# Threshold attention and a bilinear feed-forward layer on one core: transposes, normalisation and the read-back of turned weights put elsewhere in the slot

## The chip, the cores and the metric

The kernel runs on 1 core of one Trainium2 chip. The metric is the device time of one execution in microseconds (us), and the median of several executions is compared. Its engines are TensorE (PE in the profile; PEld is its weight load), VectorE (DVE), ScalarE (ACT), GpSimd (POOL) and SyncE (SP), which issues the DMA transfers. Each engine has its own list of instructions and works through it in order.

## What is computed

The first half is attention with a threshold: of each row of scores only those within tau of the row's maximum count. The second half is a feed-forward layer, the product of two linear maps, followed by a third.

```python
def _attn_ref(q, k, v, tau):            # (8, 8, 576, 64) each, tau = 0.02
    scale = 1.0 / np.sqrt(q.shape[-1])
    scores = scale * np.matmul(q, k.transpose(0, 1, 3, 2))
    thresh = np.max(scores, axis=-1, keepdims=True) - tau
    scores = np.where(scores >= thresh, scores, -1000000000.0)
    scores = scores - np.max(scores, axis=-1, keepdims=True)
    attn = np.exp(scores)
    attn = attn / (np.sum(attn, axis=-1, keepdims=True) + 1e-09)
    return np.matmul(attn, v).astype(np.float32)

def _moe_ref(x, w_a, w_b, w_out):       # x (4608, 512), d_ff 1536
    a = x @ w_a
    b = x @ w_b
    return (a * b @ w_out).astype(np.float32)
```

Between the two, the heads' outputs are put side by side: (8, 8, 576, 64) becomes (4608, 512).

## The kernel before

**Tiling.** Heads go in pairs, 32 of them (4 pairs for each of 8 batches). The 576 query rows of a pair are cut into five units, `u` = 0 to 3 with 128 rows of each of the two heads (two tiles `sc` of 128 x 576 scores) and `u` = 4 (`NT`) with the last 64 rows of both heads in one tile. That makes 160 units. Rows of `x` are gathered into blocks of 256, and each block is a piece of feed-forward work, a Python generator (`ffn`) that issues matmuls step by step.

**Slots.** The main loop (L877) has one slot `g` for each unit and three more. The Python order of a slot is the order on every engine: `keep_order` (L39) ties each instruction to the one before it on its engine. In slot `g`, for `g` > 8 (`BY_PE`), come one after the other:

- `scores` (L335): the matmuls of unit `g` into `sc`, then on VectorE the maxima `mx` (L354) and the thresholds `thr` (L355);
- `turn_blocks` (L436) for unit `g` - 1: VectorE transposes the normalised weights `tw` in place in blocks of 32 x 32 (L441), and SP writes them in four transfers to `swap`, a scratch tensor in DRAM (L452);
- `advance(PORTIONS[0] * pace)`: 30% of the slot's feed-forward matmuls;
- `weigh` (L365): ScalarE makes the exponentials out of `sc` (L374, L375), VectorE masks and sums them (L378), which frees the PSUM buffers of `sc`;
- transposes of coming q and k (`prep`), then `advance(PORTIONS[1] * pace)`: another 35%;
- in every second or third slot the product with v: `make_room`, then `weighted` (L528), whose matmuls (L478) read the turned weights `wT` of unit `g` - 3 and of the one before it; `settle` (L482) copies the result out, first ScalarE (L485), then VectorE (L487);
- `turn_back` (L455) for unit `g` - 2: SP reads the whole of `swap` into `wT` (L461). `wT` has two buffers, so it waits until the product before has read its own;
- `convert_first` (L227), while weights are still being converted (until about 155 us of the span): two operations of ScalarE for each piece of a weight matrix;
- `reciprocal` (L383, VectorE, L389 and L391; while weights are converted ScalarE adds the small constant, L387) and `normalise` (L394, ScalarE, L397);
- loads of coming q, k and v, stores, and the other 35% of the feed-forward matmuls.

**Joins.** Each feed-forward tile in PSUM is copied out by ScalarE or combined by VectorE (L629 to L645, L689, L691, L467, L468), in the order in which its matmuls were issued.

**Buffers.** All tiles in PSUM, scores, feed-forward and products, share four buffers of two banks (`banks`, L126). `tw` has three buffers, `swap` three, `wT` two.

The first eight units go another way (`turn_pe`: TensorE transposes, and the normalisation is part of it); the change doesn't touch them.

Of the kernel before, what the change touches and what calls it, by code (L numbers as in the profile page):

```python
# [23 lines left out]
BY_PE = 8  # L24
# [28 lines left out]
def kernel(  # L53
# [278 lines left out]
    def prep_copy(mT, tp):  # L332
        nc.vector.tensor_copy(mT.rearrange("p (c k) -> p c k", c=2), tp)

    def scores(i, u):  # L335
        qT, kT = prepared[i]["q" if i < HP else "q1" if u > 1 else "q0"], prepared[i]["k"]
        base = HALF if i >= HP and u > 1 else 0
        n = 2 if u < NT else 1
        sc = [banks(SH, "sc") for _ in range(n)]
        each = [(c, t, j) for c in range(2) for t in range(n) for j in range(2)]  # L340
        if units.index((i, u)) < BY_HEAD:
            each.sort(key=lambda x: x[2])
        for c, t, j in each:
            r = slice(j * D, (j + 1) * D)
            o = t if u < NT else 1 - j
            q0, to = (u * P + t * D if u < NT else MAIN) - base, slice(o * D, (o + 1) * D)
            nc.tensor.matmul(sc[j if u < NT else 0][to, c], qT[r, q0:q0 + D],  # L347
                             kT[r, c * SH:(c + 1) * SH], start=True, stop=True)
        mx = small.tile([P, 2], FP32, tag="mx", name="mx")
        thr = small.tile([P, 2], FP32, tag="thr", name="thr")  # L350
        bias = small.tile([P, 2], FP32, tag="bias", name="bias")
        for j in range(n):
            c = slice(j, j + 1)
            nc.vector.tensor_reduce(mx[:, c], sc[j], axis=AX.XY, op=ALU.max)  # L354
        nc.vector.tensor_scalar(thr[:, 0:n], mx[:, 0:n], cut, None, op0=ALU.subtract)  # L355
        scored[i, u] = (sc, thr, bias, mx)
# [37 lines left out]
    def normalise(i, u):  # L394
        ws, rcp = weights[i, u]
        for j, w in enumerate(ws):
            nc.scalar.activation(w, w, AF.Copy, scale=rcp[:, j:j + 1])  # L397
# [38 lines left out]
    def turn_blocks(i, u):  # L436

        ws, _ = weights.pop((i, u))
        t = whole.pop((i, u))
        for w in ws:  # L440
            nc.vector.transpose(w, w)  # L441
        if u < NT:
            swap = scratch.tile([G, P, NSLOT * Q], FP32, tag="swap", name="swap")
        else:
            swap = scratch.tile([2, P, NSLOT * Q], FP32, tag="swapt", name="swap")
        swaps[i, u] = swap
        for g in range(G):
            if u < NT:
                to, n = swap[g], G
            else:  # L450
                to, n = swap[g % 2, (1 - g // 2) * D:(2 - g // 2) * D], 2
            nc.sync.dma_start(to.rearrange("(r p) e -> p r e", p=Q),  # L452
                              t[g * Q:(g + 1) * Q, 0:n * NSLOT].rearrange("p (r s) e -> p r (s e)", r=n))

    def turn_back(i, u):  # L455

        swap = swaps.pop((i, u)).rearrange("g p e -> p g e")
        if u < NT or i < HP:
            turned[i, u] = turned_tile()
            n = G if u < NT else 2  # L460
            nc.sync.dma_start(turned[i, u][:, 0:n].rearrange("p g s e -> p g (s e)"), swap)  # L461
        else:
            for y in range(2):
                nc.sync.dma_start(turned[i, 2 + y][:, G].rearrange("p s e -> p (s e)"), swap[:, y])
# [343 lines left out]
    def advance(cols):  # L808
        running["owed"] += cols
        while running["owed"] > 0:  # L810
            if running["ffn"] is None:
                exchange_blocks()
                if not blocks:
                    running["owed"] = 0.0
                    return
                if len(blocks[0][0]) == 4 and state["first"] == 3:
                    first_sums(3)
                running["ffn"] = ffn(*blocks.pop(0))
                running["left"] = cost()
            step, rest, whole = next(running["ffn"], (None, 0, 0))  # L820
            if step == 0:
                running["owed"] = 0.0
                return
            if step is None:
                running["ffn"] = None
                state["through"] += 1
            else:
                running["owed"] -= step
                running["left"] -= step
                running["done"] = running["done"] + step if rest else 0  # L830
                running["rest"] = rest
                running["room"] = min(ROOM, whole // 2)
# [44 lines left out]
    for g in range(len(units) + PV_LAG):  # L877
        written = len(pending)
        state["converted"] = state["added"]
        here = g < len(units)  # L880
        converting = bool(early.get(g)) or bool(early.get(g - 1))
        if here:
            i, u = units[g]
            scores(i, u)
        exchange_blocks()
        pace = (PACE if g > BY_PE else PACE_EARLY) * BLOCK_COLS
        if g > BY_PE:
            pace = min(pace, backlog() / (min([a for a in arrivals if a > g] + [len(units) + PV_LAG + 1]) - g))
        pace += NSLOT * S / 2 / (NT + 1) + CATCH_UP * max(backlog() - BLOCK_COLS, 0)
        if 2 <= g < BY_PE + 2:  # L890
            weighted_unit(*units[g - 2])
            running["owed"] -= NSLOT * P // 2
        if g < 3:
            prep_copy(*prep_pe(g + 1, "q"))
        convert_rest(g, 0)
        if g == 3:
            for c in range(0, NSUM - 2 * CW + 1, 2 * CW):
                extra.append(sums_u32[:, c:c + 2 * CW].rearrange("p (f w) -> p f w", w=2))
        load_weights(RAWS)
        if g > BY_PE and g <= len(units):  # L900
            turn_blocks(*units[g - 1])
        if g > BY_PE:
            advance(PORTIONS[0] * pace)
        if here:
            weigh(i, u)
        if here and g < BY_PE:
            reciprocal(i, u, nc.vector)
        if 0 < g <= BY_PE:
            turn_pe(*units[g - 1])
        if g < 3:  # L910
            prep_copy(*prep_pe(g + 1, "k"))
        for p in range(HP, NPR):
            for name, d in (("q0", 2), ("k", 1), ("q1", 1)):
                if g == (second if name == "q1" else first)[p] - d:
                    prep(p, name)
        if g > BY_PE:
            advance(PORTIONS[1] * pace)
            n = g - PV_LAG
            if BY_PE <= n < len(units) and part(*units[n]):
                make_room()  # L920
                weighted(*part(*units[n]))
                running["owed"] -= NSLOT * width(*part(*units[n])) // 2
            if BY_PE + 1 < g <= len(units) + 1:
                turn_back(*units[g - 2])
        for n in early.get(g, [])[:1]:
            convert_first(n)
            convert_clamp(n)
        if here and g < BY_PE:
            diagonals(i, u)
        elif here:  # L930
            reciprocal(i, u, nc.scalar if converting else nc.vector)
            normalise(i, u)
        convert_rest(g, 1)
        if g <= BY_PE:
            advance(pace)
        convert_rest(g, 2)
        for n in early.get(g, [])[1:]:
            convert_first(n)
            convert_clamp(n)
        load_weights(RAWS)  # L940
        for p in range(HP, NPR):
            for name, d in (("q0", 4), ("k", 3), ("q1", 3)):
                if g == (second if name == "q1" else first)[p] - d:
                    load(p, name)
        for p in range(1, NPR):
            if g == first[p] - 1:
                load_v(p)
        if BY_PE <= g < BY_PE + HP:
            load_v(g - BY_PE, again=True)
        store(written)  # L950
        if g > BY_PE:
            advance(PORTIONS[2] * pace)
            advance(PORTIONS[3] * pace)

        if not converting and not state["sums"]:
            state["slots"] = state.get("slots", 0) + 1
            for n in {1: (0,), 2: (1,), 3: (2,)}.get(state["slots"], ()):
                for z in range(2):
                    weight_sums(n, z)
            if state["slots"] >= 3 and state["through"]:  # L960
                for z in range(2):
                    weight_sums(3, z)
                state["sums"] = True
        if g > first[HP] + 1 and not converting and state["first"] < 3:
            first_sums(state["first"])
# [37 lines left out]
```

## Time and profile before

| | |
|---|---|
| runs | 1473.37, 1474.51, 1476.1 us, median 1474.51 |
| profiled execution | 1469.17 us, span 1467.4 us |
| mean granted clock of TensorE | 0.996 |
| bytes read and written in HBM | 128.58 MB, 89.65 MB |
| chain that ended last | PE 81%, DVE 9%, DMA 4%, issue 2%, ACT 2% |

The groups of instructions that the change touches (name of what is written and read, number, busy us and mean ns of one; then the idle time of the engine ahead of them and what ended most of it):

| line, engine | what | number | busy, one | idle before |
|---|---|---|---|---|
| L354 DVE | mx<-sc | 288 | 205.2, 749 | 106.2, PE sc L347 |
| L441 DVE | tw<-tw | 272 | 196.0, 754 | 0.8, ACT tw L397 |
| L378 DVE | tw<-sc,thr,tw | 288 | 224.2, 800 | 14.1, ACT tw L375 |
| L397 ACT | tw<-tw,rcp | 272 | 197.8, 769 | 221.9, DVE rcp L391 |
| L375 ACT | tw<-sc,bias,scalars | 288 | 239.7, 832 | 9.9, ACT bias L374 |

And the transfers (number, KB each, median us from issue to landing): swap<-tw 480 of 144 KB, 2.6 and 128 of 72 KB, 1.8; wT<-swap 120 of 576 KB, 4.5, 56 of 144 KB, 2.6, and 4 of 288 KB, 3.3. SP waited 330.0 us for L441 before writes of swap and 102.5 us for products before reads of it.

A table of groups is read so: busy time is what an engine spends; idle time ahead of a group costs something only where another engine waits for that group in turn.

### The profile page before, as it was taken

What the parts mean: (1) busy time and instruction counts of PE and PEld (TensorE: products, weight loads), DVE (VectorE), ACT (ScalarE), POOL (GpSimd) and SP (SyncE); (2) the same over time, 40 slices, a digit from 0 to 9 for tenths busy, and PEclk for the clock granted to TensorE, in tenths of its full rate; (3) what the DMA queues carried; (4) which work ended last, traced back from release to release, by engine and by line L of the source; (5) the groups of instructions that cost most, each with busy time, mean ns of one, the idle gap of its engine ahead of it and who ended that gap; (6) DMA issues with size and microseconds to landing.
All of it is one profiled execution on the core that took longest, in us unless ns stands there. A gap on an engine that the chain in (4) does not pass through costs nothing.

```text
span 1467.4 us, 70219 instructions
## 1 busy us (share of the span) xinstructions
PE 1404.0 (96%) x31136; PEld 1224.5 (83%) x31136; DVE 1020.5 (70%) x2295; ACT 678.8 (46%) x1259; POOL 490.4 (33%) x678
## 2 busy tenths in 40 slices
PE   5779999999999999999999999999999999999998
PEld 4667687788978788899889978789898879989998
DVE  6888687778776877776757777677767786644314
ACT  5877455445544554544444545344544454331011
POOL 2764703333161606042425233241516060605000
PEclk9999999999999999999999999999999999999999
DMA  9977677678656775767545866377746776450000
GB/s 206 217 198 209 159 178 193 170 165 205 176 142 160 183 199 139 178 158 174 138 129 126 193 166 162 101 165 187 184 126 153 173 180 169 120 138 17 3 17 17
DMA packets 325056, 222.82 MB, mean 152 GB/s; under 512 B 169616, under 2 KB 308880, under 8 KB 324752
## 3 DMA queue, kind: packets, MB, share of 16 engines
q1 hardware_dynamic: 322384, 217.73, 60.1%
q8 instruction: 245, 4.01, 1.2%
q10 hardware_dynamic: 2368, 0.59, 0.2%
q14 instruction: 59, 0.48, 0.1%
HBM read 128.58 MB, written 89.65 MB: 149 GB/s over the span
## 4 chain that ended last, share of the span: by engine, by line
PE 81%; DVE 9%; DMA 4%; issue 2%; ACT 2%; SPq 1%; POOL 1%; DVEq 0%; ACTq 0%
PE pab L683 33%; PE po L728 18%; PE pab L622 11%; PE pv L478 9%; PE sc L347 9%; DVE mx L354 2%; DMA wT<-swap 2%; DVE tw L441 1%; DVE tw L378 1%; SPq L452 1%; PE po L774 1%; DVE low L255 1%; DVE xT L487 0%; POOL h L697 0%; POOL xU L502 0%
## 5 line engine op out<-in xcount | busy, mean ns | idle before, releaser
L397 ACT ACTIVATE tw<-tw,rcp 128x576 f32<-128x576 f32 x272 | 197.8, 769 | 221.9 <-DVE rcp L391 221.9
L354 DVE TENSOR_REDUCE mx<-sc 128x1 f32<-128x576 f32 x288 | 205.2, 749 | 106.2 <-PE sc L347 104.5
L375 ACT ACTIVATE tw<-sc,bias,scalars 128x576 f32<-128x576 f32 x288 | 239.7, 832 | 9.9 <-ACT bias L374 0.2
L378 DVE SCALAR_TENSOR_TENSOR tw<-sc,thr,tw 128x576 f32<-128x576 f32 x288 | 224.2, 800 | 14.1 <-ACT tw L375 13.0
L728 PE MATMUL po<-wo_sb,h 64*64 64x256 f32 x3264 | 217.0, 377 | 5.3 <-DVE t L640 5.2
L588 POOL TENSOR_TENSOR t<-u,t 128x512 f32<-128x512 f32 x14 | 17.8, 1275 | 542.1 <-ACT t L629 502.0
L441 DVE STREAM_TRANSPOSE tw<-tw 128x576 f32<-128x576 f32 x272 | 196.0, 754 | 0.8 <-ACT tw L397 0.8
L347 PE MATMUL sc<-kT,qT 64*64 64x288 f32 x2016 | 188.1, 404 | 2.4 <-DVE tw L378 1.5
L478 PE MATMUL pv<-wT,vm 64*64 64x160 f32 (+3 forms) x5184 | 183.6, 273 | 6.4 <-DMA wT<-swap 3.5
L728 PEld LDWEIGHTS po<-wo_sb,h 64*64 64x64 f32 x3264 | 159.1, 133 | 34.8 <-DVE t L640 6.4
L683 PE MATMUL pab<-xS,wa_sb 64*64 64x256 f32 (+1 forms) x2560 | 177.3, 366 | 1.8 <-issue 1.8
L478 PEld LDWEIGHTS pv<-wT,vm 64*64 64x64 f32 x5184 | 164.7, 134 | 17.0 <-issue 7.3
L683 PE MATMUL pab<-xS,wb_sb 64*64 64x256 f32 (+1 forms) x2560 | 176.2, 366 | 0.9 <-issue 0.9
L697 POOL TENSOR_TENSOR h<-h 128x256 f32<-128x256 f32 x168 | 117.7, 736 | 165.7 <-PE po L728 162.2
L683 PE MATMUL pab<-xT,wa_sb 64*64 64x256 f32 (+1 forms) x2304 | 156.1, 366 | 6.1 <-ACT wo_sb L242 1.8
L728 PE MATMUL po<-sums_u,h 64*64 64x256 f32 x2448 | 158.5, 376 | 0.6 <-DVE h L645 0.6
L683 PE MATMUL pab<-xT,wb_sb 64*64 64x256 f32 (+1 forms) x2304 | 156.9, 365 | 1.6 <-DVE h L691 1.0
L683 PEld LDWEIGHTS pab<-xS,wa_sb 64*64 64x64 f32 x2560 | 130.5, 133 | 18.9 <-issue 2.2
L683 PEld LDWEIGHTS pab<-xS,wb_sb 64*64 64x64 f32 x2560 | 131.1, 133 | 16.5 <-issue 1.6
L728 PEld LDWEIGHTS po<-sums_u,h 64*64 64x64 f32 x2448 | 118.2, 133 | 22.8 <-DVE h L645 1.0
L347 PEld LDWEIGHTS sc<-kT,qT 64*64 64x64 f32 x2016 | 111.2, 133 | 28.7 <-issue 6.3
L683 PEld LDWEIGHTS pab<-xT,wa_sb 64*64 64x64 f32 x2304 | 114.8, 134 | 22.1 <-ACT wo_sb L242 2.0
(119 smaller groups left out, 2003.8 us busy)
## 6 DMA issues: line engine op xcount, KB each, us to landing
swap<-tw SPq DMA_DIRECT2D x480, 144.0 KB, 2.6
wT<-swap SPq DMA_DIRECT2D x120, 576.0 KB, 4.5
vm<-in_v_dram SPq DMA_DIRECT2D x128, 72.0 KB, 3.1
swap<-tw SPq DMA_DIRECT2D x128, 72.0 KB, 1.8
kT<-in_k_dram SPq DMA_DIRECT2D x112, 72.0 KB, 4.3
wT<-swap SPq DMA_DIRECT2D x56, 144.0 KB, 2.6
out_dram<-kept SPq DMA_DIRECT2D x30, 256.0 KB, 4.0
raw<-in_moe_w_a_dram SPq DMA_DIRECT2D x18, 256.0 KB, 6.6
```

Of the source, the lines that this page charges most:

```text
L347: nc.tensor.matmul(sc[j if u < NT else 0][to, c], qT[r, q0:q0 + D], kT[r, c * SH:(c + 1) * SH], start=True, stop=True)
L354: nc.vector.tensor_reduce(mx[:, c], sc[j], axis=AX.XY, op=ALU.max)
L375: nc.scalar.activation(wb[j], sb[j], AF.Exp, bias=bias[:, j:j + 1], scale=e_scale)
L378: nc.vector.scalar_tensor_tensor(out=wv, in0=sb[j], scalar=thr[:, j:j + 1], in1=wv, op0=ALU.is_ge, op1=ALU.mult, accum_out=sums[:, j:j + 1])
L397: nc.scalar.activation(w, w, AF.Copy, scale=rcp[:, j:j + 1])
L441: nc.vector.transpose(w, w)
L478: nc.tensor.matmul(pv[c * D:(c + 1) * D, y], vm[rows, s], wT[y](rows, s), start=(s == 0), stop=(s == NSLOT - 1))
L588: (nc.vector if state["over"] else nc.gpsimd).tensor_tensor(*a, **kw)
L622: nc.tensor.matmul(pab[c * D:(c + 1) * D, r, y * P:(y + 1) * P], w[k][rows, w0:w0 + D], moving[k][rows], start=(k == 0), stop=(k == HP - 1))
L683: nc.tensor.matmul(pab[c * D:(c + 1) * D, r], w[rows, f // n, k, fs + c * D:fs + (c + 1) * D], moving, start=(k == 0), stop=(k == H - 1))
L697: (nc.vector if state["over"] else nc.gpsimd).tensor_tensor(*a, **kw)
L728: nc.tensor.matmul(po[c * D:(c + 1) * D, r, y], ht[rows, t0:t0 + D], other[rows, f], start=(f == 0), stop=(f == NF // 2 - 1))
```

## The change

Four edits belong together. The transposes of the unit before (`turn_blocks`, with its four writes of `swap`) are issued inside `scores`, after the matmuls and ahead of the maxima. They leave their place after `load_weights`, so their writes are now issued ahead of the loads of weights in the slot. The reciprocal and the normalisation of a unit are issued ahead of the product with v, `turn_back` and `convert_first` in slots after 8, instead of after them; slot 8 keeps the old place. And `turn_back` reads `swap` in `n` transfers, one for each group of 32 rows (four, or two for the units of 64 rows of the first four pairs), instead of one. The matmuls and GpSimd's operations keep their order.

```diff
-    def scores(i, u):
+    def scores(i, u, meanwhile):
...
             nc.tensor.matmul(sc[j if u < NT else 0][to, c], qT[r, q0:q0 + D],
                              kT[r, c * SH:(c + 1) * SH], start=True, stop=True)
+        meanwhile()
         mx = small.tile([P, 2], FP32, tag="mx", name="mx")
...
             n = G if u < NT else 2
-            nc.sync.dma_start(turned[i, u][:, 0:n].rearrange("p g s e -> p g (s e)"), swap)
+            for y in range(n):
+                nc.sync.dma_start(turned[i, u][:, y].rearrange("p s e -> p (s e)"), swap[:, y])
...
+        def turn():
+            if g > BY_PE and g <= len(units):
+                turn_blocks(*units[g - 1])
+
         if here:
             i, u = units[g]
-            scores(i, u)
+            scores(i, u, turn)
+        else:
+            turn()
         exchange_blocks()
...
         load_weights(RAWS)
-        if g > BY_PE and g <= len(units):
-            turn_blocks(*units[g - 1])
         if g > BY_PE:
             advance(PORTIONS[0] * pace)
...
         if g > BY_PE:
             advance(PORTIONS[1] * pace)
+            if here:
+                reciprocal(i, u, nc.scalar if converting else nc.vector)
+                normalise(i, u)
             n = g - PV_LAG
...
-        elif here:
+        elif here and g == BY_PE:
             reciprocal(i, u, nc.scalar if converting else nc.vector)
             normalise(i, u)
```

## The prediction

> **What bounds the kernel now.** I read the busy times first, then the table by stretches of time, then the waits of TensorE, then the order of time around two slots.
>
> ```profile
> PE 1404.0 (96%) x31136; PEld 1224.5 (83%) x31136; DVE 1020.5 (70%) x2295; ACT 678.8 (46%) x1259; POOL 490.4 (33%) x678
> ```
>
> PE is busy in 1404.0 of 1467.4 us: at most 63.4 us can be had from waits. The change leaves PE's own list as it is, so nothing else can move. The next table (stretch, length, then busy us of PE, PEld, DVE, ACT, POOL, clock, DMA) says where the 63.4 us lie.
>
> ```profile
> 0.00:62.00 62.00, 41.00 (x796) 34.13 (x796) 43.76 (x105) 39.71 (x82) 26.84 (x39) 0.94 1.08 214
> 62.00:125.00 63.00, 49.50 (x1458) 43.62 (x1459) 55.63 (x119) 46.97 (x94) 39.59 (x43) 1.00 0.84 219
> 125.00:400.00 275.00, 264.58 (x5536) 221.26 (x5537) 214.50 (x488) 147.05 (x270) 91.49 (x109) 1.00 0.71 177
> 400.00:800.00 400.00, 395.66 (x8819) 345.71 (x8819) 288.08 (x652) 188.06 (x344) 138.45 (x202) 1.00 0.63 157
> 800.00:1270.00 470.00, 461.81 (x10270) 402.39 (x10266) 338.72 (x769) 223.85 (x410) 156.75 (x230) 1.00 0.65 161
> ```
>
> 34.5 us of idle lie before 125 us, 10.4 + 4.3 + 8.2 = 22.9 us from there to 1270, the rest in the tail, which has no attention work. The change acts from slot 9 on, whose scores start at 86.5 us in the order of time. So about 23 us, and part of the 13.5 us of the second row, are in reach. The waits of PE from 125 us on (what waits, for whom: us, times, longest):
>
> ```profile
> PE po L728 <- DVE t L640: 5.2, 5, 1.7
> PE pv L478 <- DMA wT<-swap: 3.5, 3, 2.2
> PE pab L622 <- DVE h L691: 2.7, 3, 1.2
> PE sc L347 <- DVE tw L378: 2.3, 2, 1.5
> ...
> PE pab L622 <- DVE u L631: 1.8, 2, 1.1
> ```
>
> The reader is to see that the two large sorts are a join on VectorE that comes late and turned weights that come late. The order of time shows why a join can be late (start, duration; L354 maxima, L441 transposes, L378 masked sums, L389/L391 reciprocal, L487 settle):
>
> ```profile
> 531.10 0.59 DVE L487 COPY xT<-pv 64x128 f32<-64x128 f32 x2 [2.41 <-ACT xT L485]
> 531.72 0.17 DVE L389 TENSOR_SCALAR sums<-sums 128x2 f32<-128x2 f32 x1
> 531.93 0.17 DVE L391 RECIPROCAL rcp<-sums 128x2 f32<-128x2 f32 x1
> 532.01 1.40 DVE L354 TENSOR_REDUCE mx<-sc 128x1 f32<-128x576 f32 x2
> ...
> 539.18 1.42 DVE L354 TENSOR_REDUCE mx<-sc 128x1 f32<-128x576 f32 x2 [1.38 <-PE sc L347]
> 540.64 0.23 DVE L355 TENSOR_SCALAR thr<-mx,scalars 128x2 f32<-128x2 f32 x1
> 540.77 1.43 DVE L441 STREAM_TRANSPOSE tw<-tw 128x576 f32<-128x576 f32 x2
> 542.13 0.78 DVE L378 SCALAR_TENSOR_TENSOR tw<-sc,thr,tw 128x576 f32<-128x576 f32 x1
> ```
>
> There are two sorts of slot. After a slot without product VectorE sits idle for the scores (1.38 us here). After a slot with a product it comes from the settle and the reciprocal and is late itself, with no idle time.
>
> **What the Trainium skill says.** "PSUM — Partial Sum Buffer", section Engine vs sequencer instructions: the queues of ScalarE and VectorE are strict FIFO. The trace agrees: the reciprocal at 531.93 stands behind a settle that waited 2.41 us. "DMA: Bandwidth & Descriptors", section Issuing engines are not separate DMA queues: all transfers share the 16 DMA engines, so cutting one in four adds no bandwidth; its section Rules for kernel authors puts mostly overhead below 64 KB. The quarters are of 144 KB, and such ones land in 2.6 us here, the 576 KB one in 4.5.
>
> **Part 1, transposes to the front.** The same 272 x 754 ns of VectorE. In 72 waits VectorE idles 104.5 us before the maxima (L354 waits for L347), 1.45 us each: one pair of transposes (1.43 us). There they cost nothing, and what stood behind them, the joins of the first portion, comes 1.43 us earlier. The masked sums gain less, since they need the exponentials: from the maxima's start 0.79 to the first bias, then to the end of the second exponential 2.99 us (523.62 to 526.61), so the second masked sum starts at 3.0 instead of 1.42 + 0.23 + 1.43 + 0.75 = 3.8. In the other half of the slots, where VectorE is late, maxima start about 1.43 - 0.4 = 1.0 us later (0.4 is the reciprocal that left, part 2), joins 0.4 us earlier, the second masked sum 0.3 us later. Behind the transposes SP issues four writes of swap (1.76 us for four); they start 0.4 to 1.9 us earlier.
>
> The change adds a wait: the transposes now need the normalisation of the slot before, and behind them stand maxima, exponentials, and the release of the score banks. Before it is covered (L441 waited 0.8 us in all). The new round from maxima to maxima: 3.0 to the second masked sum, 1.26 from there to the normalisation (249.66 to 250.92), 0.75 for its first half, then both transposes 1.5: 6.5 us. Slots last 6 to 10.5 us; of the 142 after slot 16, 60 are under 7.8.
>
> **Part 2, reciprocal and normalisation ahead of the product.** On VectorE two small operations (0.35 to 0.4 us) leave the stretch between settle and maxima; on ScalarE 1.44 us of normalisation go ahead of the settle copy (0.27). Cover: PE's product, about 2 us. If masked sums are late the cover is gone and settle, then transposes, wait: 3.0 + 1.26 + 1.44 + 0.3 + 0.6 + 1.45 = 8.05 us for that round. With 0.6 us for one join between masked sum and reciprocal in each of the two slots, a pair then takes 6.5 + 8.05 + 1.2 = 15.75 against 15.0 for two slots of 7.5. The four PSUM buffers absorb about 1 us (an estimate: a second masked sum ends at 536.5, the next scores start at 537.8). In slots 9 to 16 ScalarE also converts weights (two to three pieces, 1.2 us each); the first piece, which filled its wait for the masked sum, now stands behind the normalisation: up to 1.2 us later per slot. Against it, the reciprocal no longer stands behind that piece (VectorE waited 1.61 us at 94.7). I take 0 for these slots; ends -2 and +6.
>
> **Part 3, four transfers.** 120 transfers become 480 (four others become eight): 364 more issues at 0.44 us = 160 us of SP's queue, 1.3 us a slot. Behind them stand loads and the writes of swap; SP issues in 64% of the densest stretch and still waits 330 us for transposes, so I cost this at nothing; without that cover a slot's writes start up to 1.3 us late, once in two slots. The last quarter is issued 1.3 us after the first and lands 2.6 later: 3.9 against 4.5. With part 1, weights are there 1 to 2.5 us earlier. PE waits on more semaphores before a product: the trace has no case; between nothing and 0.1 us for 60 products, I take 1 us, ends 0 and 5.
>
> **Sum.** Gains: of 5.2 for joins L640, the wait at 941 us lies in a slot with 1.79 us of idle (1.4), the other four give 0.35 each (1.4): 2.8. Of L691/L631 (4.5), the wait at 386 us goes whole (1.2), others 0.4: 2.4. Late weights 3.5 of 3.5. Score banks 0.5 of 2.3. Together 9.2. Losses: new round in tight slots 3 (ends 0 and 14), semaphores 1, conversion 0. Net -5.2: the profiled execution of 1469.2 us (span 1467.4) goes to about 1464. The median shown is 1474.5, 5.3 above it, and I take the same difference there: 1469.5.
>
> **Rivals.**
> 1. Stalls only move: a join that comes early lets PE run to the next bank that is not free. For it: 81% of the chain is PE, and few waits are over 1.5 us. Against it: the waits are single, with long quiet stretches between. Gain 9.2 less 3 and less half of the rest: about 1472.5 to 1475, no change.
> 2. The round decides (slower). Transposes wait at the front for ScalarE, which waits for VectorE. Price: 0.75 us for each pair of tight slots; 60 such slots are 30 pairs, 22 us, less a third that the buffers absorb: +15. Conversion adds +4, and of the gains only late weights (3.5) remain. 1474.5 + 15.5 = 1490 at full price, half of it 1482. It decides where a round with its join exceeds the slot, that is under about 7.8 us. For it: the normalisation ends up to 1.9 us after the scores in slots behind a product. Against it: that was behind the settle, and moves with part 2.
> 3. Nearly all waits in reach go (18 of 23): 1457. Against it: half the slots gain only 0.35 us.
> 4. The quarters don't start sooner than the whole, since both wait for the same release by the product (102.5 us of SP's waiting). Then 2 of the 3.5 us stay: 1471.5. It is inside the forecast.
>
> **Chances.** Forecast with rival 4: 0.42, rival 3: 0.06, rival 1: 0.20, rival 2: 0.32. What this measurement can tell from no change is 0.2%, 2.9 us. Part of the forecast lies within it, so faster is 0.44, same 0.23, slower 0.33. The range leaves out rival 3 and the dear half of rival 2: 1461 to 1486. The forecast's own range is 1464 to 1473.
>
> **What would show it.** Right: idle before L354 falls from 106 to under 50 us, and L441 waits for ScalarE or SP's wait for L441 shrinks; PE's waits for L640 fall to about 2.5 and for wT to under 1; 364 more reads of swap, landing in about 2.6 us. The forecast is wrong if L441 shows tens of us of waiting for L397, if PE waits for L378 before scores or products grow beyond 5 us, or if PE's busy time itself changes, which nothing here predicts.

## The result, and the profile after

The changed kernel takes 1501.76 us (1499.83 to 1502.21, four runs) against 1474.9 us (1473.37 to 1476.1): a ratio of 1.018, 95% interval 1.0163 to 1.0198. It is 27 us slower, where 5 us faster was forecast. The profiled execution took 1501.73 us, its span is 1499.9 us, 32.5 more than before: the profiled execution of the kernel before, at 1469.17 us, was faster than the median, so the two traces differ by some 5 us more than the medians do.

From the page of the changed kernel: the busy times, the chain that ended last, and the groups that the change touches. The functions stand one to two lines further down in this kernel: L355 are the maxima, L379 the masked sums, L442 the transposes, L398 the normalisation.

```profile
PE 1420.4 (95%) x31136; PEld 1229.5 (82%) x31136; DVE 1035.2 (69%) x2295; ACT 682.5 (46%) x1259; POOL 491.4 (33%) x678
...
PE 65%; DVE 14%; ACT 6%; DMA 6%; SPq 5%; issue 4%; POOL 0%; DVEq 0%; ACTq 0%; POOLq 0%
...
L398 ACT ACTIVATE tw<-tw,rcp 128x576 f32<-128x576 f32 x272 | 198.2, 771 | 246.6 <-DVE rcp L392 246.3
L379 DVE SCALAR_TENSOR_TENSOR tw<-sc,thr,tw 128x576 f32<-128x576 f32 x288 | 232.2, 816 | 70.8 <-ACT tw L376 53.2
...
L442 DVE STREAM_TRANSPOSE tw<-tw 128x576 f32<-128x576 f32 x272 | 197.8, 761 | 40.3 <-ACT tw L398 38.4
...
L355 DVE TENSOR_REDUCE mx<-sc 128x1 f32<-128x576 f32 x288 | 201.5, 734 | 20.3 <-PE sc L347 20.1
...
wT<-swap SPq DMA_DIRECT2D x544, 144.0 KB, 2.9
```

The chain is where to look first. PE's share of it fell from 81% to 65%; VectorE, ScalarE, transfers and SP's queue took over. The idle time ahead of the maxima fell from 106.2 to 20.3 us, as forecast. But VectorE now waits elsewhere: 70.8 us ahead of the masked sums (14.1 before) and 40.3 us ahead of the transposes (0.8 before).

The waits of TensorE after (what waits, for whom: us, times, longest), and those of SP's queue:

```profile
PE pv L480 <- DMA wT<-swap: 8.2, 7, 2.1
PE sc L347 <- issue: 7.4, 7, 2.5
...
PE sc L347 <- DVE tw L379: 5.1, 9, 1.4
PE po L730 <- DVE kept L470: 4.5, 3, 1.9
...
PE po L730 <- DVE t L642: 2.2, 3, 0.9
```

```profile
SPq L463 <- PE pv L480: 142.1, 44, 7.8
SPq L453 <- DVE tw L442: 126.5, 57, 8.0
```

The reader is to see which forecasts held and which did not: the wait for the join L640 (now L642) fell from 5.2 to 2.2 us, but the wait for turned weights rose from 3.5 to 8.2, and a new one for the join of `kept` has come. SP waits 126.5 us for transposes, where it waited 330.0, and 142.1 for products, where it waited 102.5: of 432.5 us of slack 268.6 are left.

Measured from the first scores, the score matmuls of the changed kernel fall behind by only 1.8 us up to slot 16, then by 7.6 us from slot 20 to 32 and by about as much from 120 to 132. From slot 20 on, every twenty slots make a batch of four pairs: eight slots of units `u` = 0 and 1, in which the loads of q, k and v come close together, then twelve of `u` = 2 to 4. The first twelve slots of the batches hold the whole loss from slot 20 on, 31.9 us, and the other eight none of it, -1.7 (differences between the starts of the first score matmuls in the two traces). It is the same in f_only (23.1 and -0.5) and in tn (20.0 and 1.2), two experiments that follow. VectorE's list between 245 and 255 us shows what a slot has become (start, duration, line, what is written and read; in brackets the idle time ahead and what ended it):

```profile
244.97 1.43 DVE L442 STREAM_TRANSPOSE tw<-tw 128x576 f32<-128x576 f32 x2
246.32 1.39 DVE L355 TENSOR_REDUCE mx<-sc 128x1 f32<-128x576 f32 x2
247.75 0.23 DVE L356 TENSOR_SCALAR thr<-mx,scalars 128x2 f32<-128x2 f32 x1
248.27 0.82 DVE L379 SCALAR_TENSOR_TENSOR tw<-sc,thr,tw 128x576 f32<-128x576 f32 x1 [0.30 <-DMA swap<-tw]
...
249.32 0.82 DVE L379 SCALAR_TENSOR_TENSOR tw<-sc,thr,tw 128x576 f32<-128x576 f32 x1 [0.22 <-ACT tw L376]
...
250.38 0.17 DVE L392 RECIPROCAL rcp<-sums 128x2 f32<-128x2 f32 x1
252.53 0.69 DVE L470 TENSOR_TENSOR kept<-kept,po 128x512 f32<-128x512 f32 x1 [1.98 <-ACT kept L469]
253.25 0.59 DVE L489 COPY xT<-pv 64x128 f32<-64x128 f32 x2
253.87 1.44 DVE L442 STREAM_TRANSPOSE tw<-tw 128x576 f32<-128x576 f32 x2
```

ScalarE and PE between the reciprocal and the next transposes, in the same stretch:

```profile
250.59 1.44 ACT L398 ACTIVATE tw<-tw,rcp 128x576 f32<-128x576 f32 x2 [1.30 <-DVE rcp L392]
251.93 0.56 ACT L469 COPY kept<-po 128x512 f32<-128x512 f32 x1
...
253.36 1.48 PE L730 MATMUL po<-wo_sb,h 64*64 64x256 f32 x21 [1.88 <-DVE kept L470]
```

From transposes to transposes 8.9 us pass, where a slot of this stretch had 7.3 us in the kernel before, and each step waits for the one before: transposes, maxima, exponentials, masked sums, reciprocal, then ScalarE's normalisation, ScalarE's copy for the join, VectorE's join, the settle, and the transposes again. The transposes at 253.87 have no idle time ahead of them: by then the normalisation, over at 252.0, is long done. What held them is the join. Its copy stood behind the normalisation in ScalarE's list, which itself had waited 1.30 us for the reciprocal, and PE waited 1.88 us for that join.

PE's busy time rose by 16.4 us for the same 31136 matmuls, which nothing in the forecast allowed for. The clock of this execution was 0.990 against 0.996; but an execution of the changed kernel at 0.996 took 1502.21 us, so the clock doesn't make the difference in time. It may have a part in the busy time: between 62 and 125 us PE was busy for 52.9 us at a clock of 0.89, where the same stretch before had 49.5 at 1.00, for as many matmuls. But tn, at 0.997, is 9.9 us busier than the kernel before as well. Why the rest grew stays open.

### The profile page after: what moved, and what is told of

Same layout as the page of the kernel before. It is cut to its first block, busy times and chain, and to the rows that moved or that the text cites. A ratio compares the mean times of both kernels' runs of the same rounds, so it can differ in the third digit from the quotient of the medians.

```text
span 1499.9 us, 70755 instructions
## 1 busy us (share of the span) xinstructions
PE 1420.4 (95%) x31136; PEld 1229.5 (82%) x31136; DVE 1035.2 (69%) x2295; ACT 682.5 (46%) x1259; POOL 491.4 (33%) x678
## 4 chain that ended last, share of the span: by engine, by line
PE 65%; DVE 14%; ACT 6%; DMA 6%; SPq 5%; issue 4%; POOL 0%; DVEq 0%; ACTq 0%; POOLq 0%
PE pab L685 24%; PE po L730 16%; PE pab L624 10%; PE pv L480 7%; PE sc L347 7%; DVE mx L355 3%; DVE tw L442 3%; DMA wT<-swap 3%; DVE tw L379 2%; ACT tw L398 2%; SPq L463 2%; ACT tw L376 2%; SPq L453 1%; DMA swap<-tw 1%; SPq L147 1%
## 5 line engine op out<-in xcount | busy, mean ns | idle before, releaser
L398 ACT ACTIVATE tw<-tw,rcp 128x576 f32<-128x576 f32 x272 | 198.2, 771 | 246.6 <-DVE rcp L392 246.3
L379 DVE SCALAR_TENSOR_TENSOR tw<-sc,thr,tw 128x576 f32<-128x576 f32 x288 | 232.2, 816 | 70.8 <-ACT tw L376 53.2
L442 DVE STREAM_TRANSPOSE tw<-tw 128x576 f32<-128x576 f32 x272 | 197.8, 761 | 40.3 <-ACT tw L398 38.4
L355 DVE TENSOR_REDUCE mx<-sc 128x1 f32<-128x576 f32 x288 | 201.5, 734 | 20.3 <-PE sc L347 20.1
L347 PE MATMUL sc<-kT,qT 64*64 64x288 f32 x2016 | 191.2, 405 | 10.9 <-issue 4.9
L375 ACT ACTIVATE bias<-mx,scalars 128x1 f32<-128x1 f32 x288 | 83.8, 291 | 234.9 <-DVE mx L355 234.6
```

Of the source, the lines that this page charges most:

```text
L375: nc.scalar.activation(bias[:, j:j + 1], mx[:, j:j + 1], AF.Copy, scale=e_nscale)
L379: nc.vector.scalar_tensor_tensor(out=wv, in0=sb[j], scalar=thr[:, j:j + 1], in1=wv, op0=ALU.is_ge, op1=ALU.mult, accum_out=sums[:, j:j + 1])
```

## The experiments

All are timed beside the kernel before, at 1472 to 1473.4 us in these comparisons. A ratio is to that, with its 95% interval.

### Which of the edits costs

Each of the three parts alone, then the first two together. The edits are hunks of the change: `f_only` keeps the loop over four transfers, `t_only` the call of `turn_blocks` inside `scores`, `n_only` the early `reciprocal` and `normalise`, `tn` those two.

> The kernel before with one edit alone: the turned weights are read in four transfers. Theory R (the round: transposes ahead of the maxima tie each slot's maxima to the normalisation of the slot before) expects no change, 1472 to 1478 us. Theory Q (the queue: the added issues fill SP's queue, writes of swap come late) expects most of the 27 us here, 1490 to 1502 us, with SP's issue in the slots of the densest stretches at 80% or more.

> The kernel before with one edit alone: the transposes ahead of the maxima; normalisation stays behind the product. R expects at least the loss of the whole change, 1500 to 1525 us, since the normalisation that the transposes now wait for still stands behind the settle. Q expects 1472 to 1480 us.

> The kernel before with one edit alone: reciprocal and normalisation ahead of the product. R expects 1470 to 1476 us (nothing waits for the normalisation early). A third theory, M (join copies and settle on ScalarE stand behind the normalisation and come late by themselves), expects 1480 to 1490 us.

> The change without the four transfers: transposes ahead of the maxima and normalisation ahead of the product, one transfer. R expects 1492 to 1502 us, Q 1472 to 1480 us. In between would say that both have a share.

| | us | ratio |
|---|---|---|
| f_only | 1497.75 | 1.0174 (1.0133 to 1.0215) |
| t_only | 1521.57 | 1.0322 (1.0292 to 1.0353) |
| n_only | 1480.9 | 1.006 (1.0041 to 1.008) |
| tn | 1490.58 | 1.0123 (1.0094 to 1.0153) |
| whole change | 1501.76 | 1.018 (1.0163 to 1.0198) |

Every part loses, and the losses don't add up: 25, 49 and 8 us alone, 27 together. In `t_only`, with the normalisation still behind the settle, the transposes wait for it 115 times, 89.7 us in all (tn: 54 times, 38.3 us). That fits the reason why part 2 was to go with part 1; no experiment tests how much of the 49 us this wait carries.

### The four transfers: SP's queue

SP's list in f_only, from its order of time (start, time spent in issuing, what is issued, how many):

```profile
203.34 1.83 SPq L453 DMA_DIRECT2D swap<-tw  x4
205.27 2.54 SPq L463 DMA_DIRECT2D wT<-swap  x4
207.85 1.92 SPq L147 DMA_DIRECT2D qT<-in_q_dram  x4
209.87 3.01 SPq L453 DMA_DIRECT2D swap<-tw  x4
212.97 1.88 SPq L463 DMA_DIRECT2D wT<-swap  x4
214.89 2.94 SPq L147 DMA_DIRECT2D kT<-in_k_dram  x4
217.87 2.01 SPq L170 DMA_DIRECT2D vm<-in_v_dram  x4
219.99 1.83 SPq L453 DMA_DIRECT2D swap<-tw  x4
```

So it goes on to 238.44 us, sixty issues in 35.1 us without a wait. In the kernel before, one read of 0.4 us stood in place of four of about 2.5, and SP had gaps of 1.3 to 3.8 us in this stretch:

```profile
217.56 0.40 SPq L461 DMA_DIRECT2D wT<-swap  x1
219.86 1.82 SPq L452 DMA_DIRECT2D swap<-tw  x4
...
230.01 0.39 SPq L461 DMA_DIRECT2D wT<-swap  x1
234.23 1.76 SPq L452 DMA_DIRECT2D swap<-tw  x4
```

TensorE pays for it in f_only, where its wait for turned weights has grown by 15.3 us from the 3.5 before:

```profile
PE pv L480 <- DMA wT<-swap: 18.8, 15, 2.8
```

If the queue is the cause, fewer issues or another queue for the loads must give the time back. `two_transfers` reads `swap` in two halves. `four_loads_moved` is f_only with the loads of q and k in the slots issued from GpSimd's queue (336 of them); `loads_moved`, the control, moves the same loads in the kernel before.

```diff
-                    load(p, name)
+                    load(p, name, nc.gpsimd)
```

> The kernel before with the turned weights read in two transfers in place of one. Theory Q (SP's queue is full where loads cluster) expects a third of the added issues of the four-transfer kernel and less than a third of its 25 us, since idle time of SP is used up first: 1472 to 1481 us. If smaller pieces of DRAM reads cost by themselves, half of it or more: 1485 us and up.

> The kernel before with four transfers, and the 336 loads of q and k issued from GpSimd's queue in place of SP's. Q expects most of the 25 us back: 1468 to 1480 us, with SP's waits for L442 over 300 us again. If the four transfers cost on the DMA engines or on TensorE's semaphores, it stays at 1490 to 1500 us.

> The kernel before with the loads of q and k issued from GpSimd's queue: the control for the run with four transfers. Q expects 1466 to 1474 us, since SP has idle time with one transfer and little is to be had; slower than 1478 would say that issues on GpSimd's queue cost by themselves.

> The whole change, with the loads of q and k issued from GpSimd's queue. S and Q together expect the queue's part of the change to go and the rest to stay: about the change without four transfers (1491), so 1488 to 1497 us. If the queue were all of the change's loss, 1475 to 1480 us; if it had no part, 1499 to 1505 us.

| | us | ratio |
|---|---|---|
| two_transfers | 1473.8 | 1.0012 (1.0001 to 1.0024) |
| four_loads_moved | 1478.29 | 1.0046 (1.002 to 1.0072) |
| loads_moved | 1475.87 | 1.0028 (1.0018 to 1.0039) |
| all_loads_moved (the whole change) | 1492.82 | 1.014 (1.0118 to 1.0161) |

The queue is the cause: with the loads elsewhere the four transfers cost 2.4 us over their control instead of 25, and the intervals of the two overlap. The control itself came out above its range: to issue the loads from GpSimd's queue costs 0.28% where SP has slack. The waits of TensorE and of SP in four_loads_moved agree:

```profile
PE pv L480 <- DMA wT<-swap: 5.6, 7, 1.6
```

```profile
SPq L453 <- DVE tw L442: 349.0, 134, 6.8
```

SP has its slack back (177.7 us in f_only, 349.0 here). In the whole change the move gives back 0.4%: 9 us by the medians, 6 by the ratios. The remaining 19 us are about those of tn, 18.

### The normalisation, not the reciprocal

`reciprocal_only` issues only the reciprocal ahead of the product and leaves the normalisation in its old place.

```diff
             advance(PORTIONS[1] * pace)
+            if here:
+                reciprocal(i, u, nc.scalar if converting else nc.vector)
```

> The kernel before with only VectorE's reciprocal ahead of the product; the normalisation on ScalarE stays behind it. Theory M (the 8 us of the moved normalisation come from copies on ScalarE that stand behind it) expects 1469 to 1475 us. If the reciprocal's new place is what costs, 1479 to 1484 us.

It took 1469.13 us, ratio 0.9974 (0.9964 to 0.9984): faster than both kernels, by 4 us against the one before. n_only differs from it by the place of the normalisation alone, and is 0.9% slower. In n_only, as in the change, `make_room`, which stands ahead of the product, makes joins whose copies now queue behind the normalisation. The same slot, 28, in n_only and then in reciprocal_only:

```profile
245.83 1.44 ACT L398 ACTIVATE tw<-tw,rcp 128x576 f32<-128x576 f32 x2 [2.46 <-DVE rcp L392]
247.18 0.56 ACT L468 COPY kept<-po 128x512 f32<-128x512 f32 x1
```

```profile
243.46 0.59 ACT L467 COPY kept<-po 128x512 f32<-128x512 f32 x1 [0.49 <-PE po L728]
...
245.84 1.44 ACT L397 ACTIVATE tw<-tw,rcp 128x576 f32<-128x576 f32 x2
```

The maxima of this slot start at 240.38 and 239.97 us. In reciprocal_only the copy goes as soon as TensorE is done, and VectorE's join doesn't wait for it; in n_only it stands behind 2.46 us of waiting for the reciprocal and the normalisation itself, and the join waits 1.98 us. The next maxima come 8.7 us after these instead of 6.6.

### The transposes: their wait, their place, or the round

What remains are the 10 us by which tn is slower than n_only. Three theories: the transposes' new wait for the normalisation costs; the place ahead of the maxima costs in itself; or the whole round is too long for the slot, whatever closes it. The first trial moved the transposes to the unit two slots back, whose normalisation is long over, ahead of the maxima (`two_back`) and behind them (`two_back_behind`), with the product and the read-back a slot later.

```diff
-PV_LAG = 3
+PV_LAG = 4
...
+            if g > BY_PE + 1 and g <= len(units) + 1:
+                turn_blocks(*units[g - 2])
```

> Transposes ahead of the maxima and normalisation ahead of the product, one transfer, but the transposes at the front are those of the unit two slots back, whose normalisation ended a slot ago; reads of swap and the product follow one slot later too. Theory R (the wait for the normalisation closes a round of VectorE and ScalarE) expects the 18 us of the same kernel with the unit one slot back to go: 1468 to 1480 us, and waits of L442 for L398 under 2 us. If the place ahead of the maxima costs by itself, whatever it waits for, 1485 to 1495 us.

> Like the run with the unit two slots back, but its transposes stand behind the maxima, in the old place; all else as there, the later read and product too. Theory S (series: ahead of the maxima the transposes lengthen the run from scores to masked sums, where behind them they fill the time in which VectorE waits for the exponentials; what they wait for doesn't matter) expects about the run with normalisation moved alone: 1475 to 1486 us, and VectorE's waits for exponentials back under 25 us from 71. If the slot more of delay is what cost 24 us there, 1490 to 1500 us.

1496.69 us, 1.018 (1.0143 to 1.0217), and 1503.7 us, 1.0213 (1.0191 to 1.0235). The pair was no test: the slot of delay costs some 23 us by itself (two_back_behind against n_only), so it says little about the wait. The next two add a fourth `tw` buffer to each, to see whether the delay costs through a scarcity of it.

```diff
-TW_BUFS = 3
+TW_BUFS = 4
```

> two_back with four tw buffers in place of three: the transposes of the unit two slots back stand ahead of the maxima, so they wait for no normalisation of the slot before, and the weights stay a slot longer in tw. If the 24 us of two_back come from the scarcity of tw (masked sums that wait for a buffer that is still being written out), the fourth buffer takes most of it away: at most 1480 us. If they come from the longer way to the product or from the place itself, it stays within 4 us of two_back, at 1493 to 1501 us.

> two_back_behind with four tw buffers. If the extra slot costs through tw, it goes from 1504 us to within 4 us of n_only, 1477 to 1485 us, and stands beside two_back_4tw within 3 us. If the place ahead of the maxima itself costs 10 us, two_back_4tw is 7 to 13 us slower than this one.

1496.71 us, 1.0155 (1.0134 to 1.0175), and 1496.54 us, 1.0153 (1.0132 to 1.0175). The buffer was not the cause of most of it; it gave 0.6% to the kernel with the transposes behind and nothing certain to the other. What the delay costs stays open. With the wait gone and buffers enough, the two places stand even, which speaks against a cost of the place itself, as far as kernels that lose 23 us for another, unknown reason can show it.

`one_ahead` splits the pair: normalisation early, one transpose ahead of the maxima, the other behind the thresholds.

> Normalisation ahead of the product, one transfer, and of each pair of transposes the first ahead of the maxima, the second behind the thresholds. S expects about half way between the run with normalisation moved alone (1481) and the one with both ahead (1491): 1483 to 1489 us. If one transpose fits the idle time before the maxima, 1474 to 1482 us.

1475.26 us, 1.0017 (1.0009 to 1.0026). VectorE's waits in it (L886 is its first transpose), and in tn:

```profile
DVE tw L886 <- ACT tw L398: 38.1, 53, 0.8
DVE mx L355 <- PE sc L347: 34.1, 35, 2.3
DVE tw L379 <- ACT tw L376: 29.7, 74, 2.2
```

```profile
DVE tw L379 <- ACT tw L376: 47.7, 129, 2.2
DVE tw L442 <- ACT tw L398: 38.3, 54, 0.8
```

The wait of the transposes for the normalisation is the same in both, 38 us in 53 or 54 times, and yet one_ahead is 15 us faster, and 6 us faster than n_only. So the 38 us, as a total, do not set the price. What differs is the wait of the masked sums for exponentials: in tn no transpose is left to fill it.

Then the normalisation was taken out: `x_front` is tn without it, `x_behind` is n_only without it.

> tn without the 272 normalisations on ScalarE: the weights go to the product without having been divided by their sums, so the output is not the attention. The transposes then wait for no ScalarE operation, with everything else as in tn. If the 10 us between n_only and tn come from the transposes' wait for the normalisation, this kernel is within 3 us of x_behind. If they come from the place itself, since the transposes hold up maxima and exponentials whatever they wait for, it is 7 to 12 us slower than x_behind.

> n_only without the 272 normalisations (the output is not the attention): the partner of x_front. ScalarE loses 198 us of work and the join copies that stood behind the normalisation come 1.44 us earlier, so both theories expect it at or below the kernel before, 1464 to 1474 us. Only its distance to x_front tells them apart.

1463.53 us, 0.993 (0.9907 to 0.9952), and 1465.27 us, 0.9944 (0.9923 to 0.9966). Without the normalisation the place ahead of the maxima costs nothing. And yet the masked sums of x_front wait for the exponentials as long as those of tn:

```profile
DVE tw L379 <- ACT tw L376: 48.9, 119, 2.2
```

So the total of that wait is no price either. But in x_front ScalarE lost 198 us of work together with the wait for it. `front_spare` gives the work back and not the dependence:

```diff
-            nc.scalar.activation(w, w, AF.Copy, scale=rcp[:, j:j + 1])
+            nc.scalar.activation(spare, spare, AF.Copy, scale=rcp[:, j:j + 1])
```

> tn with the 272 normalisations written to a spare tile in place of the weights: ScalarE does the same work at the same places, but the transposes don't wait for it, and the weights go undivided to the product, so the output is not the attention. If the wait of the transposes for the normalisation carries the 10 us between n_only and tn, this kernel falls to n_only or below, 1474 to 1483 us. If it is ScalarE's load that made tn slow and its absence that made x_front fast, it stays near tn, 1487 to 1494 us.

1486.79 us, 1.0103 (1.0081 to 1.0125): just below the range for load, and well above the one for the wait. By the ratios 6 of the some 10 us between n_only and tn remain without the wait (2 to 11 by the two intervals). The wait's own share comes out at 3 us; its interval reaches from nothing to 8. Nor is the load quite the same: a pair of normalisations takes 1.58 us on the spare tile and 1.44 in tn. From its order of time:

```profile
241.60 1.38 DVE L357 TENSOR_REDUCE mx<-sc 128x1 f32<-128x576 f32 x2
...
245.85 1.58 ACT L405 ACTIVATE spare<-spare,rcp 128x576 f32<-128x576 f32 x2 [1.30 <-DVE rcp L394]
...
247.34 0.57 ACT L475 COPY kept<-po 128x512 f32<-128x512 f32 x1
...
247.94 0.69 DVE L476 TENSOR_TENSOR kept<-kept,po 128x512 f32<-128x512 f32 x1 [2.12 <-ACT kept L475]
...
249.28 1.44 DVE L449 STREAM_TRANSPOSE tw<-tw 128x576 f32<-128x576 f32 x2
...
250.64 1.38 DVE L357 TENSOR_REDUCE mx<-sc 128x1 f32<-128x576 f32 x2
```

No transpose here needs ScalarE's result, and the round is still 9.0 us, 241.60 to 250.64: it closes through ScalarE's list, where the copy stands behind the normalisation, and through VectorE's, where the join stands ahead of the transposes. The same five slots in each kernel, from the maxima of slot 25 to those of slot 30 (differences of the starts in the traces):

| kernel | normalisation ahead of the copies | transposes ahead of the maxima | us for 5 slots | ratio of the whole |
|---|---|---|---|---|
| before | no | none | 36.6 | 1 |
| reciprocal_only | no | none | 36.8 | 0.9974 |
| x_front | left out | both | 35.8 | 0.993 |
| n_only | yes | none | 38.3 | 1.006 |
| one_ahead | yes | one | 38.1 | 1.0017 |
| t_only | no, behind the settle | both | 40.6 | 1.0322 |
| front_spare | yes, on a spare tile | both | 40.9 | 1.0103 |
| tn | yes | both | 41.1 | 1.0123 |
| whole change | yes | both | 41.3 | 1.018 |

A slot of this stretch has 7.3 us before (36.6 over 5). Each of the two moves puts its own time into the round: the transposes 1.4 us, and the normalisation the 1.98 us that VectorE's join waits for the copy behind it. At 8.9 us the round of the change is too long. Six rounds of x_front, from its transposes at 206.87 to those at 251.31, average 7.4 us, the slot's own length, and ScalarE's copies there wait for TensorE again:

```profile
243.91 0.27 ACT L486 COPY xT<-pv 128x128 f32<-128x128 f32 x1 [1.35 <-PE pv L479]
...
250.09 0.58 ACT L468 COPY kept<-po 128x512 f32<-128x512 f32 x1 [0.94 <-PE po L729]
```

This is why the place costs nothing where the normalisation is left out, and some 10 us where it is ahead of the copies, most of it, by the estimates above, through the round. t_only is another case: its normalisation comes late and the transposes wait for it. The four kernels with one slot more of delay stand outside this account: they have 39.9 to 41.2 us for these slots with the transposes in either place.

### A faster version

> The kernel before with the reciprocal alone ahead of the product and the read-back in two transfers. reciprocal_only gave 0.9974 and two transfers alone 1.0012. If the two effects add up, 0.9986, about 1471 us; if the earlier weights are worth something once the reciprocal no longer stands behind the settle, below 0.9974.

1469.72 us, 0.9983 (0.997 to 0.9997): the two effects add up, and reciprocal_only, with one transfer, stays the best kernel that computes the attention.

## Why the prediction was wrong

Three steps failed. Part 3 put the added issues of SP's queue at nothing; they cost 8 to 11 us here. Part 2 priced the normalisation ahead of the copies by the settle copy alone. And the closed round of part 1 and 2 together was charged with 3 us, since its long form was taken for the exception; that and part 2 make the 18 us of tn.

**Bound.** That TensorE bounds the kernel held, and no kernel here gained more than 10 of the 23 us named as the most to be had. "Nothing else can move" held for gains only; its busy time moved too, by 16.4 us.

**Part 1.** The idle time ahead of L354 was read rightly: it fell to 20.3 us, under the 50 named. That filling it costs nothing holds alone, without a normalisation ahead of the copies (x_front against x_behind), and was wrong for the change as a whole. In their old place the transposes filled VectorE's wait for the exponentials. The estimate of the masked sums ("the second masked sum 0.3 us later") took that wait as harmless. It grew from 14.1 to 70.8 us, in a round that no longer had room for it, and one_ahead, which keeps half of the cover, loses almost nothing.

**The round.** Its parts were read rightly: 3.0 us from maxima to second masked sum (246.32 to 249.32), 1.27 from there to the normalisation. What follows was sized too small. From the normalisation at 250.59 to the transposes at 253.87 there are 3.28 us, where "6.5 us" had 0.75 and "8.05" had 2.34. The prediction had 0.6 us for a join, but between masked sum and reciprocal; here the join (0.69) comes behind the normalisation, with ScalarE's copy of 0.56 us ahead of it, which was left out, and settle and transposes wait for both. In that round the sum is 8.9 us. The graver step was the choice: 8.05 was to hold only "if masked sums are late", when the product no longer covers the normalisation, so 3 us (0 to 14) were charged. In the slot shown nothing is covered: the product's last matmul ends at about 250.0, before the normalisation begins at 250.59. And the masked sums wait for exponentials 136 times, where they waited 34 times before. Seven rounds from 205.73 to 262.04 average 8.04 us, 16.1 a pair, near rival 2's 15.75 and far over two slots of 7.3. The measured price, that of tn, is 18 us. (Of the 142 slots after slot 16, 58 are under 7.8 us by the starts of the maxima, about the 60 named; but the shortest has 4.8 us and not 6.)

**The new wait.** L441 behind L397 was expected to be the sign of failure, "tens of us". It came, 38.4 us, and it was not the price: one_ahead has the same 38 us, and without the wait front_spare keeps about 6 of the 10 us. The sign was near the true round, but the round doesn't need it.

**Part 2.** The reciprocal alone was worth 4 us. The normalisation ahead of the product was given the product's 2 us as its cover and was priced on ScalarE by the settle copy alone; `make_room`'s joins were not counted. It cost 13 us by the ratios of n_only and reciprocal_only. The strict order that the prediction cites, and applies to the reciprocal, holds for these copies just as well, as slot 28 shows, and was not applied to them. In the slots of conversion 0 (-2 to +6) was right: 1.8 us up to slot 16 for everything.

**Part 3.** "So I cost this at nothing" was the second failure. The 160 us of issues were worked out rightly, and the slack of 330 us was an average. Its support, that SP issues in 64% of the densest stretch, was a misreading: summed from SP's order of time before, it issues in 86% of the 60 us from 455 to 515. Five reads of swap stand there; three issues more for each at 0.57 us would be 8.6 us, an estimate, and 8.4 were idle. The sixty issues from 203.34 to 238.44 us in f_only took 34 us, 0.57 each and not 0.44, and 35.1 us are 4.8 slots of 7.3: 12.5 issues a slot, 7.1 us, and nothing left over. The Trainium skill, "DMA: Bandwidth & Descriptors", section Issuing engines are not separate DMA queues, says that issuing from several engines "will only save the time on the sequencer it takes to initiate the DMA, which is usually small relative to the DMA itself". One issue is small here too, 0.57 us against 2.9 to land; but sixty in a row were the bound, and moving 336 to another queue was worth 19 us in f_only. The last quarter was to land 3.9 us after the first issue; issued 1.9 us after it (three quarters of 2.5), and 2.9 to land, it is 4.8, no better than the 4.5 of the whole. The extra semaphores before the products were not tested by themselves; four_loads_moved, which has them all, lost 2.4 us against its control.

**Sum and rivals.** Of the gains, 9.2 us, the join L640 came in (3.0 of 2.8), L691 and L631 gave 0.7 each, 1.4 of 2.4, late weights became a loss of 4.7, and the score banks gave nothing. Rival 2 had the right form, a closed round in tight slots, and its full price of 1490 us is what tn measured. In part that is luck: the 4 us for conversion did not come, and the wait of transposes for ScalarE that it names is not what closes the round. It had a chance of 0.32, since late masked sums were taken for the exception. The other 8 to 11 us, SP's queue, were in no rival.

## What to carry to other kernels

Before work is moved into an engine's idle time, ask what it covered where it was, and sum the closed round of a slot through every engine's list in order, copies for joins included: the margin is the slot's length less that round, and two moves that each fit may not fit together. A queue's slack is to be read in the densest two slots, not as an average: count its issues there and multiply by the time of one. And a wait that a change adds is a sign, not a price; a kernel with the same wait and another length of round tells them apart.

## What the runs showed that was not expected

- The four transfers cost 25 us alone and 8 to 11 on top of tn (by ratios and by medians). Slower slots leave SP's queue more time; that this is the reason was not tested.
- One more slot between normalisation and product cost 23 us with three `tw` buffers and 14 to 16 with four (two_back_behind and two_back_behind_4tw against n_only). The cause was not found.
- Issuing the loads of q and k from GpSimd's queue cost 0.28% in the kernel before and gave back 1.3% in f_only.
